# A decode attention block on one core: the load ring moved to byte 4096 of its partitions, and output weight rows 65,792 bytes apart

## The chip, the core and the metric

The kernel runs on one core of a Trainium2 chip. A core has five engines with instruction streams of their own (TensorE for matmuls, VectorE, ScalarE, GpSimd, and SyncE, which here issues the loads), an on-chip memory of 128 partitions that all of them work from, and 16 DMA engines that move data between it and the chip's large memory. What is measured is the device time of one execution in microseconds; the number given for a kernel is the median of several runs.

## What is computed

Two sequences, each with one new token, go through an attention block with a cache of 8192 keys and values in each of 32 heads, and then through a dense block with a squared ReLU. All data is float32.

```python
B, Sq, D = 2, 1, 512
H, Sk, Dh = 32, 8192, 128        # k_cache, v_cache: (B, H, Sk, Dh)
F = 1792

x = A_x
q = layernorm(x) @ wq                              # to (B, H, 1, Dh)
p = softmax(q . k_cache * Dh ** -0.5)
h = x + (p . v_cache) @ wo                         # wo: (H * Dh, D)
r = max(layernorm(h) @ w1 + b1, 0)
out = h + (r * r) @ w2 + b2
```

The two caches are 2 x 2 x 32 x 8192 x 128 float32 numbers, 537 MB, and every one is used once.

## The kernel before

**The ring.** One large tile, `ring`, takes all loads but the small one of `x`: three slots of 16,384 float32 numbers (65,536 bytes) in each partition, and behind them `BIAS` numbers more. `place(u)` is slot u, and `slot(i)` the slot in which head i of 64 (32 heads of two sequences) lies. The first half of a slot holds the head's keys, the second its values. In the large memory the array `kvd` has one row of 65,536 bytes for each head and partition, so a head is 128 rows, 8 MB, and one DMA.

The weights use the ring too. The query weights `WQ` come first, into slot 2. Towards the end the output weights `WO` go into slot 2, and `W1` and `W2` of the dense block into slot 0. The row of the output weights in the large memory (`wod`) is 16,384 numbers and then `BIAS` = 32 more, the biases b1 and b2 of the dense block (18 numbers) and zeros; the last piece of `WO` that is loaded takes these with it, to the end of the ring (`load_wo`). So in memory the rows of `wod` begin (16,384 + 32) x 4 = 65,664 bytes apart.

**Placing of tiles.** `sb(name, shape)` takes the next free bytes of all partitions, in the order of the calls. `ring` is the first tile that the function asks for, and lies at byte 1152, behind constants that the system placed there. The small tiles follow as they come up in the code: `xr`, `ident`, `fold`, `pick` and so on up to `res`.

**The order of the work.** Before the loop, `x` is normalised, the queries of all heads are computed and copied into 32 columns each. Then a loop runs over the first 60 heads, three in a turn (line 328 for SyncE, from line 339 for the others). For a head, TensorE waits for its load (`kv_full`) and computes the scores (line 347) into one of two halves of the accumulation memory; VectorE takes their maximum (line 353), ScalarE the exponentials (line 359), VectorE multiplies the values with them in place in the ring, with a running sum, in four parts (line 364), and copies the results to `ALL` (line 368), after which the slot is free (`kv_free`). SyncE waits for that (line 318) and issues the load of the head three further on into the same slot.

The last four heads and the rest are written out, recorded by the class `Line`, which works out the waits between engines from the tiles that each operation reads and writes; all its operations have lines of helpers (137 load, 140 matmul, 144 activation, 162 the fused multiply, 166 reduction). It lets SyncE have at most 7 loads in flight. The last loads are, in order: the first half of `WO`, the last two heads in pieces, the other 16 parts of `WO` as 10 and 6 with the end of the last head's values behind them, `W1` in two pieces and `W2` in four. `pick`, `fold` and `ident` are constants used as matmul operands; `OT` holds the attention outputs, transposed, as operand of the output projection. The result leaves through the tile `res` (line 608).

Of the kernel before, what the change touches and what calls it, by code (L numbers as in the profile page):

```python
# [10 lines left out]
P = 128  # L11
NQ = 4
# [5 lines left out]
BH = H * B  # L18
# [6 lines left out]
W1_PIECES = [2, 2]  # L25
WO_PIECES = [10, 6]
EARLY = 7
BIAS = 32
W2_PIECES = [5, 5, 3, 1]
OUT = P - 32 + B  # L30
AHEAD = 8
# [143 lines left out]
def attention_block_kernel(nc, xd, kvd, wqd, wod, w1d, w2d, out):  # L175
    def sb(name, *shape):
        return nc.alloc_sbuf_tensor(name, [P, *shape], F32).ap()
# [6 lines left out]
        nc.alloc_semaphore(n) for n in ("s_full", "m_full", "e_full", "v_done", "kv_free", "s_free"))  # L184


    ring = sb("ring", SLOTS * ROW + BIAS)

    def place(u):
# [32 lines left out]
    line.memset(eps_t, EPS)  # L222
    zero = sb("zero", 1)
    line.memset(zero, 0.0)
    ident = sb("ident", P)
    line.memset(ident, 0.0, "pool")
    line.op("pool", lambda e: e.affine_select(out=ident, in_=ident, compare_op=ALU.not_equal, fill=1.0, base=0,
                                              pattern=[[-1, P]], channel_multiplier=1), [ident], [ident])
# [15 lines left out]
    def summed(src):  # L244
        line.reduce(part, src.rearrange("p d b -> p b d"), ALU.add)
        return part
# [30 lines left out]
    line.copy(xn, cols[:, :, 1])  # L277
    warm = sb("warm", 1)
    line.act(warm, eps_t, AF.Exp)
    fold = sb("fold", 32)  # L280
    line.reduce(fold, quads.rearrange("p j m -> p m j"), ALU.add)
    pick = sb("pick", NQ, P)
    line.copy(pick, quads[:, :, :1].to_broadcast([P, NQ, P]))
    pick_all = sb("pick_all", P)
    line.copy(pick_all, fold[:, :1].to_broadcast([P, P]))
# [22 lines left out]

    ALL = sb("ALL", BH, ST)
    NM, LS, AC = ALL[:, :, 0], ALL[:, :, 1], ALL[:, :, 2:]  # L310
    OT = sb("OT", BH)
    st3 = sb("st3", SLOTS, ST)

    line.op("pe", lambda e: e.wait_ge(s_free, 2), [q3, QR], [S[0], S[1]])
# [113 lines left out]
    def joined(n, pl, po):  # L428
        a, b = g_at[n]
        nb = b - a  # L430
        line.reciprocal(rl[:, :nb], pl[:, :nb])
        line.tensor(OT[:, a:b], po[:, :nb], rl[:, :nb], ALU.mult)

    rows = big[:, :D]

    def project(hs, hp):

        for h in hs:
            j = h % NQ
            line.matmul(hp[32 * j : 32 * j + B, :], OT[:, h * B : (h + 1) * B], WO[:, h, :],  # L440
                        start=(h < NQ), stop=(H - 1 - h <= NQ))
# [16 lines left out]
    def load_wo(a, b):  # L458

        cut = slice(a * D, b * D + (BIAS if b == H else 0))  # L460
        line.load(ring[:, 2 * ROW :][:, cut], wod[:, cut])
# [106 lines left out]
    line.matmul(pm, ones_d, summed(hT))  # L568
    line.copy(OT[:, a:b], po[:, :B])
    line.tensor(xc, hT, pm[:, None, :].to_broadcast([P, DB, B]), ALU.subtract)  # L570
    line.tensor(hT, hT, b2T[:, :, None].to_broadcast([P, DB, B]), ALU.add)
    ph = sums[:, 256 : 256 + DB * B].rearrange("p (d b) -> p d b", b=B)
    for d in range(DB):
        line.matmul(ph[:, d, :], woc[:, d * P : (d + 1) * P], OT[:, a:b])
    line.tensor(xc, xc, ph, ALU.add)
# [21 lines left out]
    for m in range(FB):  # L597
# [3 lines left out]
        if m == W2_PIECES[0] - 1:  # L601
            for j in range(NQ):
                at = o[32 * j : 32 * j + B, :]
                line.matmul(at, hT[:, j, :], ident, start=False, stop=False)
                line.matmul(at, OT[:, BH - B :], WO[:, H - 1, j * P : (j + 1) * P], start=False, stop=False)
    res = sb("res", P)
# [38 lines left out]
```

## Time and profile before

| | us |
|---|---|
| median of 3 runs | 1303.5 (1303.44 to 1303.68) |
| profiled execution, span from first to last instruction | 1302.0 |
| TensorE busy in it | 410.3 |
| VectorE busy in it | 742.1 |
| ScalarE busy in it | 143.8 |

The profile has the times of every instruction of one execution, and of every packet of its DMAs. "q" behind an engine's name means its sequencer, which issues DMAs and waits on semaphores. A group of instructions is named by the line that issued it, the engine and the operation, then the tile written, an arrow, and the tiles read. A stage is a stretch of the span with the busy time of each engine in it, the number of instructions in brackets, the TensorE clock granted, the mean busy share of the 16 DMA engines and the rate that they moved. In the timeline an instruction stands with its start and duration; in brackets behind it, how long the engine had been idle and what ended the wait. A DMA issue stands with its size and the time from issue to landing. Addresses are not in the profile.

### The profile page before, as it was taken

The page shows a single profiled execution, that of the slowest core. Times are in us where ns is not written, and L with a number is a line of the kernel's source. Part 1 is how long each engine was busy: PE and PEld are TensorE (multiplying, and loading weights), DVE is VectorE, ACT ScalarE, POOL GpSimd, SP SyncE. Part 2 cuts the span into 40 slices and gives each one's busy share as a digit, 9 for nine tenths or more (in the row PEclk, how much of TensorE's full clock was granted, in tenths as well). Part 3 has the DMA queues.
Part 4 walks back from the last instruction along what each step waited for, and adds up shares of the span by engine and source line. Part 5 has one row for each costly group of instructions (what it writes and reads, how often), then busy time and mean ns, then how long its engine had stood idle before and what let it go on. Part 6 is the DMA issues. An engine that isn't in the chain of part 4 may idle for free. (4 is left out here: it accounts for less than half of the span.)

```text
span 1302.0 us, 6678 instructions
## 1 busy us (share of the span) xinstructions
PE 410.3 (32%) x2418; PEld 110.0 (8%) x2418; DVE 742.1 (57%) x704; ACT 143.8 (11%) x149; POOL 0.7 (0%) x6
## 2 busy tenths in 40 slices
PE   1423223223313323323313322322322332331337
PEld 0100000000000000000000000000000000000113
DVE  1355665655665564665565565566566466556554
ACT  1011010111011011011011011001101101101111
POOL 0000000000000000000000000000000000000000
PEclk9766566666566566656656566656656665656668
DMA  9999999999999999999999999999999999999998
GB/s 419 420 443 427 443 427 443 425 441 429 429 437 425 443 427 443 427 443 425 441 429 431 439 421 445 425 443 427 443 425 443 427 431 439 425 441 425 430 428 369
DMA packets 11359, 561.16 MB, mean 431 GB/s; under 512 B 1266, under 2 KB 1364, under 8 KB 1880
## 3 DMA queue, kind: packets, MB, share of 16 engines
q1 hardware_dynamic: 11352, 561.07, 99.7%
q8 instruction: 4, 0.07, 0.0%
q14 instruction: 3, 0.02, 0.0%
HBM read 561.01 MB, written 0.05 MB: 431 GB/s over the span
## 5 line engine op out<-in xcount | busy, mean ns | idle before, releaser
L364 DVE SCALAR_TENSOR_TENSOR ring<-ring,s 128x2048 f32<-128x2048 f32 x240 | 534.7, 2282 | 136.2 <-DVEq L318 136.2
L347 PE MATMUL s<-ring,q 128*32 128x512 f32 x1920 | 346.6, 888 | 805.0 <-PEq L318 805.0
L353 DVE TENSOR_REDUCE st<-s 128x1 f32<-128x2048 f32 x60 | 137.5, 2291 | 327.7 <-DVEq L318 327.7
L359 ACT ACTIVATE s<-s,st 128x2048 f32<-128x2048 f32 x60 | 116.5, 1942 | 1034.0 <-ACTq L318 1034.0
L347 PEld LDWEIGHTS s<-ring,q 128*32 128x32 f32 x1920 | 87.6, 156 | 1063.2 <-issue 1063.2
L162 DVE SCALAR_TENSOR_TENSOR ring<-ring,s 128x2048 f32<-128x2048 f32 x15 | 33.6, 2282 | 7.2 <-ACT s L144 7.2
L140 PE MATMUL s<-ring,QR 128*32 128x512 f32 x128 | 23.0, 884 | 39.8 <-DMA ring<-in_kvd 26.3
L166 DVE TENSOR_REDUCE ALL<-s 128x1 f32<-128x2048 f32 x4 | 9.2, 2292 | 21.3 <-PE s L140 21.3
L364 DVE DVE_READ_ACCUMULATOR ring<-ring,s 128x1 f32 x240 | 19.7, 82 | 0.0
L368 DVE TENSOR_SCALAR ALL<-st 128x6 f32 x60 | 10.3, 171 | 15.1 <-DVEq L318 15.1
L144 ACT ACTIVATE s<-s,ALL 128x2048 f32<-128x2048 f32 x4 | 7.8, 1942 | 51.7 <-DVE ALL L166 51.7
L166 DVE TENSOR_REDUCE sx<-xr 2x1 f32<-2x512 f32 x1 | 0.7, 675 | 21.5 <-DMA xr<-in_xd 21.5
L359 ACT ACTIVATION_READ_ACCUMULATOR s<-s,st 128x1 f32 x60 | 11.6, 193 | 0.0
L140 PE MATMUL s<-ring,OT 128*2 128x512 f32 (+1 forms) x70 | 9.7, 555 | 1.6 <-DMA ring<-in_wod 1.6
L140 PE MATMUL s<-ident,xr 128*128 128x4 f32 x8 | 1.9, 356 | 26.2 <-DVE xr L158 26.2
L140 PEld LDWEIGHTS s<-ring,QR 128*32 128x32 f32 x128 | 5.2, 156 | 56.7 <-DMA ring<-in_kvd 28.1
L140 PE MATMUL s<-ring,xn 128*2 128x512 f32 x64 | 9.1, 729 | 0.3 <-DVE xn L151 0.3
L140 PE MATMUL s<-ring,xc 128*2 128x448 f32 (+1 forms) x34 | 8.0, 946 | 1.4 <-DMA ring<-in_w1d 1.4
L158 DVE TENSOR_SCALAR QT<-s 128x64 f32<-128x64 f32 x1 | 0.2, 225 | 10.1 <-PE s L140 10.1
L144 ACT ACT_TABLE_LOAD x4 | 5.1, 1283 | 0.8 <-PEq L637 0.7
L355 DVE TENSOR_SCALAR q<-QT 128x96 f32 x20 | 4.8, 242 | 0.0
L140 PE MATMUL s<-lw,pick_all 128*128 128x62 f32 (+1 forms) x4 | 1.1, 355 | 10.8 <-DVE lw L154 10.8
(81 smaller groups left out, 53.6 us busy)
## 6 DMA issues: line engine op xcount, KB each, us to landing
ring<-in_kvd SPq DMA_DIRECT2D x3, 4096.0 KB, 32.2
ring<-in_wod SPq DMA_DIRECT2D x1, 4096.0 KB, 28.2
ring<-in_w1d SPq DMA_DIRECT2D x2, 1792.0 KB, 37.3
ring<-in_kvd SPq DMA_DIRECT2D x1, 3072.0 KB, 29.1
ring<-in_wod SPq DMA_DIRECT2D x1, 2560.0 KB, 34.9
ring<-in_w2d SPq DMA_DIRECT2D x2, 1280.0 KB, 29.2
ring<-in_wod SPq DMA_DIRECT2D x1, 1552.0 KB, 38.1
ring<-in_kvd SPq DMA_DIRECT2D x2, 512.0 KB, 37.9
```

The source lines that it names most:

```text
L140: self.op("pe", lambda e: e.matmul(out, lhsT, rhs, start=start, stop=stop), [lhsT, rhs], [out])
L144: self.op("act", lambda e: e.activation(out, in_, func, bias=bias, scale=scale, accum_out=accum_out), [in_, *more], [out] + ([] if accum_o ...
L158: self.op("dve", lambda e: e.tensor_scalar(out, in_, by, None, op0=ALU.mult), [in_, *more], [out])
L162: self.op("dve", lambda e: e.scalar_tensor_tensor(out, a, by, b, op0=op0, op1=op1, accum_out=accum_out), [a, b, *more], [out] + ([] if acc ...
L166: self.op("dve", lambda e: e.tensor_reduce(out, in_, axis=AX.X, op=op, negate=negate), [in_], [out])
L347: made = pe.matmul(bk[n][32 * j : 32 * j + 32, :], q3[:, u, :], keys(u)[:, j, n * BLK : (n + 1) * BLK], start=True, stop=True)
L353: dve.tensor_reduce(nm, s, axis=AX.X, op=ALU.max, negate=True).then_inc(m_full, 1)
L355: dve.tensor_scalar(q3, QT[:, bass.ds(i0 + SLOTS, SLOTS), None].to_broadcast([P, SLOTS, 32]), 1.0, None, op0=ALU.mult)
L359: act.activation(s, s, AF.Exp, bias=nm, scale=1.0, accum_out=ls).then_inc(e_full, 1)
L364: made = dve.scalar_tensor_tensor(v, v, 1.0, s, op0=ALU.mult, op1=ALU.mult, accum_out=st3[:, u, 2 + e : 3 + e])
L368: dve.tensor_scalar(ALL[:, bass.ds(i0 + u, 1)], st3[:, u : u + 1], 1.0, None, op0=ALU.mult).then_inc(kv_free, 1)
```

## The change

`BIAS` becomes 64, so a row of `wod` is (16,384 + 64) x 4 = 65,792 bytes; the numbers added are zeros, and the ring becomes 32 numbers longer at its end. Four small tiles, `pick`, `ident`, `OT` and `fold`, are asked for ahead of the ring; with 2048, 512, 256 and 128 bytes a partition they move the ring from byte 1152 to byte 4096. What is written to these tiles, and when, is as it was.

```diff
-BIAS = 32
+BIAS = 64
...
+    pick = sb("pick", NQ, P)
+    ident = sb("ident", P)
+    OT = sb("OT", BH)
+    fold = sb("fold", 32)
     ring = sb("ring", SLOTS * ROW + BIAS)
...
-    ident = sb("ident", P)
     line.memset(ident, 0.0, "pool")
...
-    fold = sb("fold", 32)
     line.reduce(fold, quads.rearrange("p j m -> p m j"), ALU.add)
-    pick = sb("pick", NQ, P)
     line.copy(pick, quads[:, :, :1].to_broadcast([P, NQ, P]))
...
-    OT = sb("OT", BH)
```

## The prediction

> **What bounds the kernel now.** I read the page's slices and DMA queues first, then the stages, then TensorE's timeline inside the loop and at the end. The slices and the queue row:
>
> ```profile
> span 1302.0 us, 6678 instructions
> ...
> PE 410.3 (32%) x2418; PEld 110.0 (8%) x2418; DVE 742.1 (57%) x704; ACT 143.8 (11%) x149; POOL 0.7 (0%) x6
> ...
> DMA  9999999999999999999999999999999999999998
> DMA packets 11359, 561.16 MB, mean 431 GB/s; under 512 B 1266, under 2 KB 1364, under 8 KB 1880
> ...
> q1 hardware_dynamic: 11352, 561.07, 99.7%
> ```
>
> No compute engine is busy for much more than half of the span, while the DMA engines work in every slice and the one load queue fills 99.7% of them. So the time is the byte count over the rate, plus a start and an end. The long middle, as stages and as a DMA view of the same stretch:
>
> ```profile
> core 0: us, PE busy (x) PEld busy (x) DVE busy (x) ACT busy (x) POOL busy (x), PEclk, DMA share, GB/s
> ...
> 100.00:1100.00 1000.00, 301.44 (x1664) 76.01 (x1664) 587.62 (x531) 107.01 (x104) 0.00 (x0) 0.62 1.00 433
> ...
> DMA packets 7432, 433.33 MB, mean 433 GB/s; under 512 B 820, under 2 KB 820, under 8 KB 820
> ...
> ring<-in_kvd SPq DMA_DIRECT2D x52, 37.5
> ```
>
> 7432 less 820 small ones are 6612 packets with 433.33 MB, so 65,536 B each: one packet is one whole row of one partition. One K and V load has 128 of them, 8 for each of 16 engines. The period of a load can be had more finely from TensorE, which starts each head when its load has landed:
>
> ```profile
> 82.09 3.64 PE L347 MATMUL s<-ring,q 128*32 128x512 f32 x16 [13.80 <-PEq L318]
> ...
> 1185.11 5.85 PE L347 MATMUL s<-ring,q 128*32 128x512 f32 x32 [14.06 <-PEq L318]
> ```
>
> Between these starts lie 57 heads: (1185.11 - 82.09) / 57 = 19.351 us for 8,388,608 B, 433.5 GB/s, or 2418.9 ns for a packet on its engine. Against that period TensorE computes for about 6 us, and VectorE spends 587.62 of 1000 us. A load takes 37.5 us from issue to landing, nearly two periods, so each is issued some 18 us before its own transfer begins. That is the cover for everything that the compute engines do in the loop. The end:
>
> ```profile
> 1298.85 1.21 PE L140 MATMUL s<-ring,a 128*2 128x128 f32 x32 [0.51 <-DMA ring<-in_w2d]
> 1300.10 0.29 DVE L151 COPY res<-s 128x128 f32<-128x128 f32 x1 [4.63 <-PE s L140]
> 1300.42 0.36 SPq L608 DMA_DIRECT2D out<-res  x1
> ```
>
> The last weights land, 1.2 us of matmuls, a copy and the store follow: about 3 us in which loading is over.
>
> **The change part by part.** No instruction is added, removed or reordered. Three things differ: where in a partition the ring begins, how long a row of the output weights is, and where the small tiles lie.
>
> *The price that is open: a packet's fixed part.* An address can act on the rate per byte or on a fixed cost per packet. The trace separates them, since the weights at the end have shorter rows than K and V:
>
> ```profile
> ring<-in_wod SPq DMA_DIRECT2D x1, 4096.0 KB, 28.2
> ring<-in_w1d SPq DMA_DIRECT2D x2, 1792.0 KB, 37.3
> ...
> ring<-in_wod SPq DMA_DIRECT2D x1, 2560.0 KB, 34.9
> ...
> ring<-in_wod SPq DMA_DIRECT2D x1, 1552.0 KB, 38.1
> ...
> 1275.95 2.74 PE L140 MATMUL s<-ring,OT 128*2 128x512 f32 x20 [0.87 <-DMA ring<-in_wod]
> ...
> 1279.69 1.88 PE L140 MATMUL s<-ring,OT 128*2 128x512 f32 x10 [0.69 <-DMA ring<-in_wod]
> ...
> 1282.00:1289.00 7.00, 5.43 (x44) 3.15 (x44) 2.62 (x12) 0.21 (x1) 0.00 (x0) 0.73 1.00 426
> ```
>
> The last two pieces of the output weights land 3.74 us apart by their matmuls, and the second is 1552 KB, 12,416 B a row: 3.74 / 8 = 467.5 ns a packet. With the 2418.9 ns of 65,536 B, a straight line gives 1951.4 ns for 53,120 B, 27.22 B/ns an engine or 435.5 GB/s for 16, and a rest of 467.5 - 456.1 = 11.4 ns a packet. The stage from 1282 to 1289 carries W1 rows of 14,336 B at 426 GB/s: 538.4 ns a packet, and by the same reckoning a rest of 12.0 ns. (The semaphore writes that close each load are in this rest.) The whole kernel has (11359 - 1266) / 16 = 631 packets an engine of that queue, nearly all into the ring. So all that a better address could remove of the fixed part is 631 x 11.4 = 7.2 to 7.6 us.
>
> *The ring at byte 4096.* 1152 is 128 past a multiple of 256 and of 512; 4096 is a multiple of both and of 4096. The ends: no effect, 0; everything fixed gone, -7.6 us; above zero I find no end in a row, since every load before has the same offset, so I take the rival's price below, +10 us. I choose 0. The reason is the line itself. If the write side cut each row into badly placed pieces at a cost for each piece, that cost would come at irregular points only if the pieces were long against 12,416 B; three row lengths, from 12,416 to 65,536 B, lie on one line with the same rest. So what a bad start costs, if anything, comes once for a packet, in the 11.4 ns, or is a constant share of the 27.22 B/ns, which no row here can split. [...]
>
> *The rows of the output weights.* Each row gets 32 more float32 zeros, 128 B, in 128 rows: 16,384 B, and they are loaded with the last piece (1552 KB becomes 1568). At 433.5 GB/s that is +0.04 us on the path. The pitch was 65,664, which puts every second row 128 B past a multiple of 256; it will be 65,792, a multiple of 256. Were 128 B wasted for each such row, 64 rows in three loads, that would be 24,576 B, 0.06 us: the ends are -0.06 and 0. I take 0, because the 12,416 B rows, half of them so placed, have a rest of 11.4 ns and the W1 rows, none of which are, 12.0 ns. The sum of this part is +0.04 us. The two tensors that follow in memory move by 16,384 B, a multiple of their former alignment; 0.
>
> *The small tiles.* `pick`, `ident`, `OT` and `fold` now lie ahead of the ring, the rest behind it moves up. Their instructions keep shapes and order. In the loop they are not used; before the loop and at the end they run while loads are under way, and the matmuls with `ident` and `OT` end before TensorE waits 0.51 us for the last of W2 (row at 1298.85). What is uncovered is that row's 1.21 us and the copy's 0.29. A tenth longer or shorter would be 0.15 us either way; I take 0.
>
> Sum: 0 + 0.04 + 0 + 0 on the profiled 1302.0 us, and the median of 1303.5 lies 1.5 above this span, so 1303.5.
>
> [...]
>
> **The rivals.** *First, a piece of 128 B a packet is saved.* Place: the start of every packet into the ring. Price: 128 B at 27.22 B/ns are 4.7 ns, times 631 are 3.0 us: 1300.5. For it: a rest of 11.4 ns is there, and 4.7 fits into it. Against it: the weights' rows with source starts of both kinds show no step. That is weak evidence, because 4.7 ns in four of eight packets would be 0.02 us of 3.74, near the row's last digit. The limit of this rival, the whole rest gone, gives 1303.5 - 7.2 = 1296.3; it needs packets and semaphore writes that follow each other without any gap, so it gets little.
>
> *Second, slower: source and destination meet their block limits together.* K and V rows begin at multiples of 65,536 in memory. Before, the destination reached a multiple of 4096 some 2944 B, 108 ns by 27.22 B/ns, after the source did; after the change both reach it in one moment. If a pause on one side was absorbed while the other side ran on, and now both pause, an engine loses, say, one 32 B step, 1.18 ns, at each 4096 B. With 561.07 MB over 16 engines these are 8561 limits, 10.1 us: 1313.6. It decides from 0.31 ns a limit (2.6 us of 8561). Against it: no such pause is to be seen in a line whose rate per byte is the same for short and long rows, and the DMA share is already 1.00.
>
> *Third, the change does not do what it says:* another tile could be placed ahead, so that the ring lies elsewhere. The four tiles named have 2048 + 512 + 256 + 128 = 2944 B, just the difference of 4096 and 1152, so this is unlikely, and by time alone it could not be told from no change: 1303.5.
>
> **How the numbers follow.** No effect, the third rival included: 0.61. The first rival: 0.22 at about 1300.5, and 0.04 for more than that. The second: 0.13. A measurement of this kernel tells about 0.2%, 2.6 us, from no change. So faster is 0.22 + 0.04 = 0.26, same 0.61, slower 0.13. The likeliest is 1303.5. The range leaves out most of the slower rival and the limit of the first, together some 0.17: down to 1299.7, a little below the first rival, and up to 1305.0, where the slower one begins at 0.2 ns a limit.
>
> **What would show it.** Right: the same 19.35 us between TensorE's starts in the loop, 433 GB/s from 100 to 1100 us, and the last W2 matmuls near 1298.9. The first rival: a period shorter by 8 x 4.7 = 38 ns, 19.31 us, and the short rows of W1 and W2 at a visibly higher rate (14,336 B in 533.7 ns, 430 GB/s). The second: a longer period, 128 limits an engine and load times its price (19.50 us at 1.18 ns), with the DMA share still 1.00. If instead the period stays and the time moves, the cause is at the start or the end, and the waits before the first head and after 1260 us show where; then the step on the small tiles is wrong.

## The result, and the profile after

| | before | after |
|---|---|---|
| median, us | 1303.51 (17 runs) | 1301.18 (17 runs) |
| profiled span, us | 1302.0 | 1299.6 |

The changed kernel takes 0.9982 of the time before, with a 95% interval of 0.9976 to 0.9988: 2.33 us less. The forecast was 1303.5, no change. Its range (1299.7 to 1305.0) holds the time, but the kernel did become faster, by close to the 0.2% that the prediction had set as the least change to be told from none.

The page of the changed kernel, the same rows as before the change (engines, slices and queue row):

```profile
span 1299.6 us, 6678 instructions
...
PE 418.8 (32%) x2418; PEld 113.0 (9%) x2418; DVE 742.1 (57%) x704; ACT 143.8 (11%) x149; POOL 0.7 (0%) x6
...
DMA  9999999999999999999999999999999999999998
...
DMA packets 11359, 561.17 MB, mean 432 GB/s; under 512 B 1266, under 2 KB 1364, under 8 KB 1880
...
q1 hardware_dynamic: 11352, 561.08, 99.8%
```

The packets are as many as before and the 16 KB of zeros show as 0.01 MB; the queue is as full as it was. VectorE and ScalarE are busy as long as before; TensorE is busy 418.8 us where it was 410.3, still a third of the span. What has changed is the rate in the long middle, 434 GB/s where it was 433, in the row of that stage (columns as in the stages shown before):

```profile
100.00:1100.00 1000.00, 307.23 (x1664) 77.21 (x1664) 590.45 (x534) 107.00 (x104) 0.00 (x0) 0.62 1.00 434
```

and in the DMA view of the same 1000 us:

```profile
DMA packets 7444, 434.11 MB, mean 434 GB/s; under 512 B 820, under 2 KB 820, under 8 KB 820
```

In 1000 us 7444 - 820 = 6624 large packets started where 6612 did: 12 more, 0.18%, the same share as the gain in time. TensorE's first and last start of the same 57 heads (timeline of the changed kernel):

```profile
82.25 3.64 PE L347 MATMUL s<-ring,q 128*32 128x512 f32 x16 [13.70 <-PEq L318]
...
1183.32 5.20 PE L347 MATMUL s<-ring,q 128*32 128x512 f32 x32 [12.99 <-PEq L318]
```

(1183.32 - 82.25) / 57 = 19.317 us a head, against 19.351. The first of these heads starts 0.16 us later than before, the last 1.79 us earlier, so the loop gave 1.95 us. The end of the timeline:

```profile
1296.64 1.10 PE L140 MATMUL s<-ring,a 128*2 128x128 f32 x32 [0.47 <-DMA ring<-in_w2d]
1297.78 0.29 DVE L151 COPY res<-s 128x128 f32<-128x128 f32 x1 [4.47 <-PE s L140]
1298.10 0.36 SPq L608 DMA_DIRECT2D out<-res  x1
```

The wait for the last of W2 ends 2.21 us earlier than before. The matmuls behind it take 1.10 us where they took 1.21, so copy and store come 2.32 us earlier. So the loads go a little faster, in the loop and after it, and the end of the kernel follows them.

### The profile page after: what moved, and what is told of

Read it like the earlier page. It is cut to its first block, busy times and chain, and to the rows that moved or that the text cites. A ratio compares the mean times of both kernels' runs of the same rounds, so it can differ in the third digit from the quotient of the medians.

```text
span 1299.6 us, 6678 instructions
## 1 busy us (share of the span) xinstructions
PE 418.8 (32%) x2418; PEld 113.0 (9%) x2418; DVE 742.1 (57%) x704; ACT 143.8 (11%) x149; POOL 0.7 (0%) x6
## 5 line engine op out<-in xcount | busy, mean ns | idle before, releaser
L347 PE MATMUL s<-ring,q 128*32 128x512 f32 x1920 | 353.2, 903 | 796.0 <-PEq L318 796.0
```

What stands on the lines that cost most here:

```text
L347: made = pe.matmul(bk[n][32 * j : 32 * j + 32, :], q3[:, u, :], keys(u)[:, j, n * BLK : (n + 1) * BLK], start=True, stop=True)
```

## The experiments

All kernels are compared by two numbers: the time, and the period of a head in the loop, which is the difference of the two TensorE starts shown, over 57. A head starts when the last of the 16 engines' parts has landed, so either end can lie some hundredths of a microsecond off: the starts of every third head (the same slot) lie within 0.011 us of a straight line in the trace of before, and in that of the changed kernel within 0.03 us, but for the first, which is 0.07 off. A second reading of the period leans on no single start: all the large packets of the loop that start from 100 to 1100 us in the kept trace are put in order of time, and a straight line is laid through their starts. It gives 19.351 us a head for the kernel before and 19.319 for the changed one, 32 ns where the two starts give 34; where the two readings differ, this one is taken. Kernels with the ring at the same place below agree to 0.001 us in either. The loads of the loop are K and V alone. Lines of the code move by one to four where tiles or loops were added.

### Which part of the change does it

The changed kernel with the rows of the output weights as before:

```diff
-BIAS = 64
+BIAS = 32
```

> The ring at byte 4096, the output weights' rows still 65,664 bytes apart. Theory A (the start of each packet in the ring decides): the period of a load in the loop is that of the changed kernel, 19.32 us, and the time 1301.2 within 0.2. Theory B (the row distance has part in it): the loop as changed too, but the end longer, 1301.4 or more, by up to 0.3 us.

```profile
82.09 3.64 PE L347 MATMUL s<-ring,q 128*32 128x512 f32 x16 [13.51 <-PEq L318]
...
1183.15 5.40 PE L347 MATMUL s<-ring,q 128*32 128x512 f32 x32 [12.78 <-PEq L318]
```

1301.06 us (ratio to before 0.9982, 0.9973 to 0.9991), and (1183.15 - 82.09) / 57 = 19.317 us: the whole gain. Then the other part alone, the kernel before with `BIAS = 64`:

```diff
-BIAS = 32
+BIAS = 64
```

> The ring at byte 1152, the output weights' rows 65,792 bytes apart. Theory A: period 19.35 us as before, time 1303.5 within 0.2. Theory B: loop as before, the end shorter by 0.1 to 0.3 us, 1303.2 to 1303.4. Neither lets the loop change.

```profile
82.53 2.79 PE L347 MATMUL s<-ring,q 128*32 128x512 f32 x12 [14.36 <-PEq L318]
...
1185.52 5.31 PE L347 MATMUL s<-ring,q 128*32 128x512 f32 x32 [12.91 <-PEq L318]
```

1303.58 us (1.0001, 0.9992 to 1.0010) and 19.351 us: nothing. The distance of the weights' rows is without effect that can be seen, with the ring in either place.

### The ring's address or the small tiles

The kernel before with `BIAS = 64` and an unused tile ahead of the ring; the four small tiles stay behind it.

```diff
+    sb("pad", 32)
     ring = sb("ring", SLOTS * ROW + BIAS)
```

> An unused tile of 128 bytes ahead of the ring, which then begins at byte 1280: a multiple of 256, not of 512, 1024 or 4096; the small tiles stay behind the ring. Theory A with 256 as the unit: 19.32 us a load, 1301.2. Theory A with 512 or more as the unit: 19.35, 1303.5. Theory C (the place of the small tiles decides, the ring's does not): 19.35, 1303.5.

```profile
82.36 3.64 PE L348 MATMUL s<-ring,q 128*32 128x512 f32 x16 [13.76 <-PEq L319]
...
1183.41 5.16 PE L348 MATMUL s<-ring,q 128*32 128x512 f32 x32 [13.04 <-PEq L319]
```

1301.11 us (0.9983, 0.9974 to 0.9992) and 19.317 us: a multiple of 256 is as good as one of 4096. The opposite case has the same unused tile in the changed kernel, behind its four small tiles:

> The changed kernel with an unused tile of 128 bytes between its four small tiles and the ring: byte 4224, 128 past a multiple of 4096. Theory A: the gain is gone, 19.35 us a load and 1303.5. Theory C: the four tiles still lie ahead, so 19.32 us and 1301.2.

```profile
82.09 3.64 PE L348 MATMUL s<-ring,q 128*32 128x512 f32 x16 [14.29 <-PEq L319]
...
1185.11 5.36 PE L348 MATMUL s<-ring,q 128*32 128x512 f32 x32 [12.85 <-PEq L319]
```

1303.53 us (1.0000, 0.9991 to 1.0010) and 19.351 us: the gain is gone. The two together show that the ring's first byte decides, and the small tiles' place does not. Theory C falls.

### What a start off the boundary costs

If the cost were a count of bytes, another distance from the boundary would change it. The same unused tile with 160 bytes, and in a second kernel with 352 (88 in place of 40):

```diff
+    sb("pad", 40)
     ring = sb("ring", SLOTS * ROW + BIAS)
```

> 160 unused bytes ahead of the ring: byte 1312, 32 past a multiple of 256. Theory A1 (each packet that starts between two multiples of 256 costs one piece more, wherever it starts): 19.35 us a load as at 128 past, 1303.5. Theory A2 (it costs the bytes between the multiple below and its start, as 32 B steps of 1.18 ns): one step in place of four, 8 x 1.18 = 9 ns a load over the changed kernel's 19.319, so 19.328 and 1301.8.

```profile
82.44 3.59 PE L348 MATMUL s<-ring,q 128*32 128x512 f32 x13 [13.32 <-PEq L319]
...
1185.94 5.25 PE L348 MATMUL s<-ring,q 128*32 128x512 f32 x24 [13.81 <-PEq L319]
```

> 352 unused bytes ahead: byte 1504, 224 past a multiple of 256. Theory A1: 19.35 us, 1303.5. Theory A2: seven steps, 66 ns a load over 19.319, so 19.385 us and 1305.4. A third reading, A3 (the bytes from the start to the next multiple count): one step, 19.328 and 1301.8, and seven steps with the ring at 1312.

```profile
82.44 3.59 PE L348 MATMUL s<-ring,q 128*32 128x512 f32 x13 [12.88 <-PEq L319]
...
1185.94 5.35 PE L348 MATMUL s<-ring,q 128*32 128x512 f32 x24 [13.37 <-PEq L319]
```

Both have (1185.94 - 82.44) / 57 = 19.360 us, and 1304.25 and 1304.29 us (1.0005, 0.9995 to 1.0014, and 1.0006, 0.9996 to 1.0016). Both byte counts, A2 and A3, with an estimate of 1.18 ns for 32 B from the 27.22 B/ns, wanted the two far apart: 19.328 and 19.385 in one order or the other. A1 has it right that they are equal, but not that they are equal to 128 past. There the period is 19.351. So a second, smaller step exists. By time alone it could not be told from nothing, as both intervals hold 1; it rests on the periods, which agree. Two more places look for it, byte 1216 (`sb("pad", 16)`) and byte 1296, 16 past a multiple of 256; the latter by a slice that leaves out the first 4 numbers of the tile:

```diff
+    sb("pad", 32)
-    ring = sb("ring", SLOTS * ROW + BIAS)
+    ring = sb("ring", SLOTS * ROW + BIAS + 4)[:, 4:]
```

> Ring at byte 1216, 64 past a multiple of 256. If the extra over 128 past comes with every start that is not a multiple of 128: 19.359 us a load, 1304.3, as at 32 and 224. If it comes only with starts that are not a multiple of 64: 19.350, 1303.5.

1216 is 4 x 256 + 192, so it is 192 past a multiple of 256 (64 short of the next) and not 64 past, as the expectation says. What the run is for holds all the same: 1216 is a multiple of 64 and not of 128.

```profile
82.27 3.64 PE L348 MATMUL s<-ring,q 128*32 128x512 f32 x16 [14.37 <-PEq L319]
...
1185.45 5.21 PE L348 MATMUL s<-ring,q 128*32 128x512 f32 x32 [13.00 <-PEq L319]
```

> Ring at byte 1296, 16 past a multiple of 256 and off the 32 byte grid, which the tiles keep by themselves. 32 and 224 past have 19.359 us a load, 128 past 19.350. Theory A1 with a step for starts that are not a multiple of 128: 19.36 us, 1304.3. Theory D (a start off the grid of 32 bytes shifts every step of the write): visibly more, 19.37 us or above.

```profile
82.27 3.20 PE L348 MATMUL s<-ring,q 128*32 128x512 f32 x16 [13.31 <-PEq L319]
...
1186.32 4.98 PE L348 MATMUL s<-ring,q 128*32 128x512 f32 x24 [14.09 <-PEq L319]
```

192 past: 1303.61 us (1.0001, 0.9991 to 1.0011); its 19.354 us lies between the others, but the time is that of 128 past (1303.53 and 1303.58) and not that of 32 past, and the line through all packets gives 19.351 us a head, as for 128 past (19.351) and not as for 32 (19.360). 16 past: 1304.95 us (1.0012, 1.0002 to 1.0022) and 19.369 us. In a table:

| first byte of the ring, past a multiple of 256 | us a head, two starts | us a head, all packets | time, us |
|---|---|---|---|
| 0 (1280, 4096) | 19.317 | 19.319 | 1301.06 to 1301.18 |
| 128 (1152, 4224) | 19.351 | 19.351 | 1303.51 to 1303.58 |
| 192 (1216) | 19.354 | 19.351 | 1303.61 |
| 32, 224 (1312, 1504) | 19.360 | 19.360 | 1304.25, 1304.29 |
| 16 (1296) | 19.369 | 19.369 | 1304.95 |

A first step of some 32 ns a head comes with each of the starts tested off a multiple of 256, and about 9 ns more for each of the two finer grids that the start leaves, 64 and then 32. These places leave a second reading open: they lie 128, 64, 32, 32 and 16 bytes from the nearest multiple of 256, and the cost rises as this distance falls. A start 96 past, off the grid of 64 but far from a multiple of 256, would tell the two apart; it was not run, and the grid of 32 rests on one place. Theory D, which wanted 19.37 or above, is met by size, but its kind, a cost for every step of the write, is not what came: 9 ns a head are 1.2 ns for each of the 8 packets, and rows of other lengths, under "Once for a packet, or a share of the bytes", show that this too comes once.

### The other end of the transfer

Rows of K and V in the large memory are put 65,792 bytes apart and begin 128 past a multiple of 256. First with the ring at 4096:

```diff
+SKIP = 32
...
+    kvd = kvd[:, :, SKIP : SKIP + ROW]
...
-        "kvd": np.concatenate([k, v], axis=2),
+        "kvd": np.pad(np.concatenate([k, v], axis=2), ((0, 0), (0, 0), (SKIP, 64 - SKIP))),
```

> The changed kernel, ring at 4096, with the K and V rows in the large memory 65,792 bytes apart and beginning 128 past a multiple of 256. Theory W (only where the write begins counts): 19.32 us, 1301.2. Theory R (a start off the boundary costs the reading side as much): 19.35 us or a little more, 1303.5. Theory S (the two starts have to agree): 19.35 us.

```profile
81.95 3.63 PE L349 MATMUL s<-ring,q 128*32 128x512 f32 x17 [13.25 <-PEq L320]
...
1183.00 5.66 PE L349 MATMUL s<-ring,q 128*32 128x512 f32 x32 [14.21 <-PEq L320]
```

Then the same with the ring at 1152:

> Ring at 1152 and the K and V rows 128 past a multiple of 256 too, 65,792 bytes apart: both starts are off by the same 128. Theory W: 19.35 us as with the ring alone off, 1303.5. Theory R: both sides cost, 19.35 if they overlap, up to 19.38 and 1305.5 if they add. Theory S (starts have to agree): 19.32 us and 1301.2.

```profile
82.18 3.64 PE L349 MATMUL s<-ring,q 128*32 128x512 f32 x16 [12.78 <-PEq L320]
...
1185.16 5.20 PE L349 MATMUL s<-ring,q 128*32 128x512 f32 x32 [13.02 <-PEq L320]
```

1301.17 us (0.9981, 0.9971 to 0.9990) and 19.317; 1303.58 us (1.0000, 0.9990 to 1.0009) and 19.351. Theory W holds: of the two places, only that of the write shows in the time. A read that begins 128 bytes further on costs nothing that shows (what it might cost behind the write could not be seen), and two starts that agree help nothing.

### Once for a packet, or a share of the bytes

The kernel before and the changed kernel, each with the whole K and V loads issued as two of half a row, so that the same bytes come in twice the packets:

```diff
-            sp.dma_start(slot(u), kvd[...].rearrange("o p c -> p (o c)")).then_inc(kv_full[u], 16)
+            for c in (slice(0, HALF), slice(HALF, ROW)):
+                sp.dma_start(slot(u)[:, c], kvd[...].rearrange("o p c -> p (o c)")[:, c]).then_inc(kv_full[u], 16)
...
-            take(pe, kv_full[u], 16)
+            take(pe, kv_full[u], 32)
```

> The kernel before (ring at 1152), with each whole K and V load issued as two of half a row, 32,768 bytes: 16 packets an engine and head in place of 8, the same bytes. To be read against the same split with the ring at 4096. Theory P (a start off the boundary costs once for a packet): the two splits differ by 16 x 3.94 = 63 ns a head, twice the 31.6 of whole rows, so this one has about 19.43 us a head and the kernel 1308 us. Theory Q (it costs a constant share of the bytes): they differ by 31.6 ns as before, about 19.39 us.

```profile
82.59 2.79 PE L351 MATMUL s<-ring,q 128*32 128x512 f32 x12 [14.17 <-PEq L320]
...
1190.01 1.94 PE L351 MATMUL s<-ring,q 128*32 128x512 f32 x8 [13.22 <-PEq L320]
```

> The changed kernel (ring at 4096) with the same split. What is left of the fixed part is known from whole rows only together with the semaphore write, (19319 - 524288 / 27.2) / 8, some 5 ns a packet; so 8 packets more give about 19.36 us a head and 1304 us. Theory P: 63 ns less than the split with the ring at 1152. Theory Q: 31.6 ns less.

```profile
82.20 3.64 PE L351 MATMUL s<-ring,q 128*32 128x512 f32 x16 [13.58 <-PEq L320]
...
1185.80 5.78 PE L351 MATMUL s<-ring,q 128*32 128x512 f32 x32 [14.11 <-PEq L320]
```

(1190.01 - 82.59) / 57 = 19.428 us and 19.361 us: they differ by 67 ns a head, where whole rows differ by 34; by all packets it is 65 (19.427 and 19.362) where whole rows differ by 32. By time, 1308.17 (1.0035, 1.0023 to 1.0048) less 1303.64 (1.0002, 0.9992 to 1.0011) is 4.53 us, against 2.33. Theory P holds: the cost comes once for a packet. That the split was carried out as meant is seen in the DMA view of the middle of the second of them:

```profile
DMA packets 14868, 433.10 MB, mean 433 GB/s; under 512 B 1651, under 2 KB 1651, under 8 KB 1651
...
ring<-in_kvd SPq DMA_DIRECT2D x104, 4096.0 KB, 32.0
```

14868 - 1651 = 13217 packets for 433.10 MB, 32,768 B each.

The traces of the kernel before and the changed one hold another witness, the weights and the last heads, whose rows are shorter. The mean recorded time of a packet, by the bytes of its row:

| bytes of the row | packets | before, ns | after, ns |
|---|---|---|---|
| 4096 | 256 | 161.4 | 159.0 |
| 10,240 | 256 | 388.5 | 385.0 |
| 14,336 (`W1`) | 256 | 540.2 | 535.0 |
| 24,576 | 128 | 915.5 | 912.0 |
| 65,536 | 8064 | 2423.1 | 2419.9 |

The differences, 2.4 to 5.2 ns, do not grow with the length, while a share of the bytes would make the last sixteen times the first. The finer steps go the same way: rows of 14,336 bytes take 541.1 ns at 32 and 224 past and 541.9 at 16 past, rows of 65,536 bytes some 2424.1 and 2425.2, again about 1 ns a step in both.

The runs with halves also measure what a packet costs besides its bytes. The split adds 8 packets an engine to each of the 62 whole K and V loads (60 heads of the loop and the next two), 496. With the ring at 1152 that is 1308.17 - 1303.5 = 4.7 us, 9.4 ns for each packet with its share of the semaphore writes (the packets under 512 B, 1651 in the view above, 32 a head, where whole loads have 820, 16 a head); with the ring at 4096 it is 1303.64 - 1301.18 = 2.5 us, 5.0 ns. By the periods of all packets the two are 9.5 and 5.4 ns. The difference, 4.4 or 4.1 ns, is the price of the bad start measured once more: 32 / 8 = 4.0 ns from the whole rows, 65 / 16 = 4.1 from the halves, and 2.33 us over 631 packets are 3.7. So it is about 4 ns.

## Why the prediction was wrong

*What bounds the kernel* was right: the queue of loads, and nothing else, in either kernel. Its period moved by 0.032 us and the time followed, while VectorE, the busiest of the compute engines, kept its 742.1 us.

*The step that failed is the choice of 0 for the ring at byte 4096.* The reason given was that three row lengths lie on one line with the same rest, so that a bad start costs, if anything, once for a packet "in the 11.4 ns", or a constant share of the rate, which the prediction says no row can split. The first of the two was right: the halved rows show it (65 ns a head against 32). But it says where such a cost must be, not that there is none. No row of before had another start, the prediction said so itself, and took the end of the range that needs no mechanism. The rest of 11.4 ns was a finding that asked for a cause; about 4 ns of it were this one. That the time still lies in the range is no merit of this step: the range's lower end was set from the first rival.

*The first rival was the case that came*, with the place right, the size a little high and the measure not quite: it put 4.7 ns on a packet and 3.0 us on the kernel; about 4 ns and 2.33 us came. Its price, 128 bytes for a start 128 past a multiple of 256, was the author's estimate: no run shows a piece of 128 bytes that is saved. The distance of the start from the multiple of 256 below is not what counts, since 32 and 224 past have the same period (19.360 us). That the first and largest step goes by 256 bytes, the runs show for the write: 1280 is as good as 4096 (19.317 us), and 1152 and 4224, 128 past, are not (19.351). Of reads moved by 128 bytes they show no cost (1301.17 us against 1301.18), and a cost behind the write would not show.

*The limit of that rival*, all the fixed part gone, did not come: 5.0 to 5.4 ns a packet remain with the ring at a multiple of 256.

*The price of a packet.* The rest of 11.4 ns, read from one short piece of weights, was too high: the halved rows give 9.4. By it the limit would have been 631 x 9.4 = 5.9 us and not 7.2. The second reading, 12.0 ns from `W1`, comes out at 11.7 by the prediction's own line (538.4 less 14,336 / 27.22), and its stage holds 11 packets of `W2` beside 200 of `W1`. The rate of the line, 435.5 GB/s, stands within 0.1%: 19.319 us less 8 x 5.4 ns leave 19.276 us for 8,388,608 B, 435.2 GB/s.

*The rows of the output weights*, 0.04 us up and at most 0.06 down, are too small to be judged by these times; the pairs of kernels that differ in them alone, 1301.06 and 1301.18, and 1303.58 and 1303.5, show nothing.

*The small tiles* were rightly put at 0: with them ahead of or behind the ring the time is the same (1301.18 and 1301.11).

*The slower rival*, limits of 4096 bytes met on both sides together, is refuted by the sign (1301.18 us where it put 1313.6), and by the ring at 1280. That both sides have such limits, with a pause at each, was the author's supposition, and no run shows one. At 1280 the destination's multiples of 4096 do not meet the source's, and the period is that of 4096. The third, that the ring lies elsewhere and nothing changes, falls with the gain, which 128 bytes more undo. Of the tests named, the period decided as it should. The rate of `W1` in its stage, 430 GB/s by the first rival, could not. It counts whole packets by where they start, and the corresponding stage of the changed kernel, with 427 where it was 426, holds 199 of `W1` and 13 of `W2` where there were 200 and 11:

```profile
1280.00:1287.00 7.00, 6.10 (x44) 3.74 (x44) 2.59 (x12) 0.17 (x1) 0.00 (x0) 0.65 1.00 427
```

The recorded times of the packets themselves, in the table above, do decide: `W1`'s fell by 5.2 ns, near the 4.7 of this rival.

*Left open:* what makes the first step about 4 ns and the finer ones about 1.1 (9 / 8), and whether the finer ones go by grids or by the distance to the nearest multiple of 256. The runs show the size, the places tested and that it is once for a packet; what goes on inside the write was not seen.

## What to carry to other kernels

In a kernel that is bound by loads, put the tile that receives them at a multiple of 256 bytes in its partitions; one unused tile of 128 bytes ahead of it did here all that the change did (1301.11 us against 1301.18). The cost comes once for a packet, so it is worth 0.18% with rows of 65,536 bytes (2.33 us) and twice as much with halves (4.53 us). The few packets of 4096 bytes at the end took 161.4 ns before and 159.0 after; by an estimate from these times and from the 4 ns of the long rows, a kernel of such rows would gain 1.5 to 2.5%, which was not run. And where a trace holds only one value of the thing that changes, a cost that no row can separate is not a reason to choose zero; an unexplained rest is a place where it may hide.

## What the runs showed of the hardware

Not expected: the first byte of the destination counts. At 128 and 192 past a multiple of 256 a load took 32 ns longer for its 8 packets an engine (19.351 against 19.319 us), at 32 and 224 past 9 ns more (19.360), at 16 past 9 more again (19.369). It came once for a packet: 2.4 to 5.2 ns in rows from 4096 to 65,536 bytes, and 65 ns a head with halved rows where whole ones gave 32. The source's first byte, moved by 128, shows no cost (1301.17 us against 1301.18).
